# Three constants of a list scheduler: the DMA rate, the hold of the shared port and the number of passes

## The chip, the cores and the metric

The kernel runs on one core of one Trainium2 chip. The metric is the device time of one execution in microseconds (us); lower is better. Engines are named as the profile names them: PE is TensorE (PEld its weight loads), DVE VectorE, ACT ScalarE, POOL GpSimd and SP SyncE, which only issues transfers.

## The reference

All tensors are float32. Attention with a threshold feeds a dense layer with `h - tanh(h)`, and that a mixture of experts with one expert for each token.

```python
# q, k, v: (4, 8, 576, 64); tau = 0.02
scores = q @ k.transpose(0, 1, 3, 2) / 8
thresh = scores.max(-1, keepdims=True) - tau
scores = np.where(scores >= thresh, scores, -1e9)
attn = np.exp(scores - scores.max(-1, keepdims=True))
attn = attn / (attn.sum(-1, keepdims=True) + 1e-9)
x = (attn @ v).transpose(0, 2, 1, 3).reshape(2304, 512)

h = x @ w_in                         # w_in: (512, 2048)
x = (h - np.tanh(h)) @ w_out         # w_out: (2048, 512)

e_idx = np.argmax(x @ w_gate, 1)     # 8 experts; gate_w is the softmax weight of e_idx
eom = 1 / (1 + np.exp(-(x @ w_output_gate)))
out[t] = gate_w[t] * eom[t, e] * (np.maximum(x[t] @ w1[e], 0) @ w2[e])   # e = e_idx[t]
# w1: (8, 512, 1024), w2: (8, 1024, 512)
```

## The kernel before

Every operation is first recorded and only later emitted. A call of `sc.add` (class `Sched`) records an engine, a duration in ns, a due time and the buffers that are read and written. `Sched.emit` then asks `Sched.order` for one order of all of them, and each engine gets its operations in that order. On the chip an engine executes its own queue strictly in that order: an operation whose input is late holds back all that stands behind it on that engine, ready or not.

`Sched.order` builds the order by list scheduling. `Sched.greedy` plays the program through forward in time on a plan of the engines and takes, whenever an engine is free, the ready operation with the best priority. Then a pass backward in time gives new priorities, and the next forward pass uses them. After `ROUNDS` such passes (8) the order with the shortest planned span is taken. The plan knows of three costs that matter here:

- A transfer (the helper `dma`) is two entries: 500 ns on the issuing queue (1038 ns for POOL) with 480 ns of latency, and `nbytes // 360` ns on a single queue "DQ", which stands for all DMA engines, with 810 ns of latency. Each step from engine to engine adds a lag (`LAG`, 170 ns where it has no entry) and a `MARGIN` of 60 ns. Without waiting in "DQ" a transfer of 512 KB is planned to land 500 + 480 + 230 + 1456 + 810 + 230 = 3706 ns after its issue begins.
- DVE operations with two operands in SBUF, DVE casts and all POOL operations but its DMAs are marked `port`. They share one planned port; the second waits until the first is through with its whole duration.
- PE runs at half speed until it has been busy for a while.

The work itself has three stages.

- Attention, 0 to about 515 us of the profile: 32 units of one batch entry, one half of its rows and one pair of heads. Each unit computes scores on PE (`sp`, L945 for the first eight units, L936 for the others), takes the minimum of the negated scores while it copies them (DVE L954, tile `em`), the exponential on ACT (L957, tile `e`), the threshold on POOL (L965), mask and sum on DVE (L967), transposes on PE (L1000), copies to `eth` and `elh` (the helper `round_to`, ACT, L416) and the product with v (`pv`, L1047). Its inputs come through SP: `kst`, `vt`, `qh` for the first batch entry, `kr`, `vr`, `qr` for the others, which are split into a rounded part (L416) and a rest (L430 on POOL, L436 on DVE).
- The dense layer, in 9 chunks of 256 tokens (L597 `ph` and L631 `x`), part of it among the attention units and the rest until about 765 us. Its weights come in pairs of tiles `wi` and `wo`. The first visit of a pair loads four packed pieces `craw` (L532, one buffer while attention runs), unpacks each on ACT (L537) and DVE (L539, L542, L545, L548) and rounds it (L416, L430); the pair is saved to DRAM (`wsv`) and fetched again later (L519, 1 MB a tile, planned with 6000 ns more latency). The router runs beside the rest of it.
- The experts, from about 785 us: POOL gathers rows (L1453) and pairs of weight tiles `wraw` (L1304, 512 KB, two buffers), ACT (L416) or DVE (L420) rounds them and DVE (L436) makes the rest; PE computes `ph` (L1517), ACT (L1522, `hh`) and DVE (L1524, `hl`) evict it, PE computes `py` (L1545), and POOL scatters the output rows (L1557).

```python
    def dma(due, fn, r, w, nbytes, eng="SP", slack=0, after=()):
        o = sc.add(eng, 1038 if eng == "POOL" else 500, due, fn, r, w, lat=480, after=after)
        if due < 0 and not after:
            opening.append(o)
        sc.add("DQ", nbytes // 360, due, lambda: None, r, w, lat=810 + slack)
```

Of the kernel before, what the change touches and what calls it, by code (L numbers as in the profile page):

```python
# [10 lines left out]
F32 = mybir.dt.float32  # L11
F32R = mybir.dt.float32r
# [30 lines left out]
    -0.003480356204087328, 0.0012444686215600763, -0.00033910333953393964, 4.8818629992721306e-05,  # L43
)
UMAX2 = 0.0016
ROUNDS = 8
PORT = True
HALVE = 400
FULL = 8
NHH = 12  # L50
ENGINES = {
# [36 lines left out]
class Sched:  # L88
# [80 lines left out]
    def greedy(self, prio, back=False):  # L169

        ops = self.ops
        n = len(ops)
        nxt, prv = (self.pred, self.succ) if back else (self.succ, self.pred)
        left = [len(p) for p in prv]
        at = [0.0] * n
        start, end = [None] * n, [None] * n
        events = [(0.0, k) for k in range(n) if not left[k]]
        heapq.heapify(events)
        ready, free, wake = {}, {}, []
        order = []  # L180
        tick, cols, warm, port = 0, 0.0, False, 0.0
        while events or wake:
            now = events[0][0] if events and (not wake or events[0][0] <= wake[0][0]) else wake[0][0]
            touched = set()
            while events and events[0][0] <= now:
                _, k = heapq.heappop(events)
                e = ops[k].eng
                heapq.heappush(ready.setdefault(e, []), (now if e == "DQ" and not back else prio[k], k))
                touched.add(e)
            while wake and wake[0][0] <= now:  # L190
                touched.add(heapq.heappop(wake)[1])
            for e in sorted(touched):
                q = ready.get(e)
                while q and (e == "-" or free.get(e, 0.0) <= now):
                    k = heapq.heappop(q)[1]
                    dur = ops[k].dur
                    if PORT and ops[k].port:
                        begin = max(now, port)
                        port = begin + dur
                        dur = port - now  # L200
                    if e == "PE" and not back:
                        t, work = now, float(dur)
                        while work > 0:
                            b = int(t // TICK)
                            if b > tick:
                                warm = b == tick + 1 and cols >= WARM
                                tick, cols = b, 0.0
                            rate = 1.0 if warm else 0.5
                            room = (b + 1) * TICK - t
                            step = min(work, room * rate)  # L210
                            cols += step
                            work -= step
                            t = (b + 1) * TICK if work > 0 else t + step / rate
                        dur = t - now
                    start[k], end[k] = now, now + dur
                    order.append(k)
                    if e != "-":
                        free[e] = now + dur
                        heapq.heappush(wake, (now + dur, e))
                    for m, lag in nxt[k]:  # L220
                        if lag is not None:
                            t = end[k] + lag
                        elif back:
                            t = max(end[k] - ops[m].dur, now)
                        else:
                            t = now
                        if t > at[m]:
                            at[m] = t
                        left[m] -= 1
                        if not left[m]:  # L230
                            heapq.heappush(events, (max(at[m], now), m))
        assert len(order) == n, (len(order), n)
        return order, start, end
# [82 lines left out]
def tile_main(ctx, tc, qa, qb, q0, kT, vv, tau, w_in, w_out, gates, w1, w2, out, dbg=None):  # L316
    nc = tc.nc
    sc = Sched()
# [120 lines left out]
    def dma(due, fn, r, w, nbytes, eng="SP", slack=0, after=()):  # L439
        o = sc.add(eng, 1038 if eng == "POOL" else 500, due, fn, r, w, lat=480, after=after)  # L440
        if due < 0 and not after:
            opening.append(o)
        sc.add("DQ", nbytes // 360, due, lambda: None, r, w, lat=810 + slack)
        return o

    TAU = 2600
# [453 lines left out]
    def attention(ui, k0, qs):  # L900
        b, half, hp = units[ui]
        n = 320 if half else 256
        full = ui < FULL
        kb, vb_ = kst[b, hp], vts[b, hp]
        qh, ql = qs
        dt_ = F32 if full else F32R
        eth = [buf("et", f"eth{h}", 1, [P, 4, 320], dt_) for h in range(2)]
        elh = buf("et", "elh", 1, [P, 320], dt_)
        if not full:
            etl = [buf("et", f"etl{h}", 1, [P, 4, 320], F32R) for h in range(2)]  # L910
            ell = buf("et", "ell", 1, [P, 320], F32R)
        T0 = k0 * TAU
        pairs = []
        k = 0
        plist = []
        rsums = []
        for qt in range(2 + half):
# [4 lines left out]
            for h in range(1 if merged else 2):  # L922
# [5 lines left out]
                e = buf("ep", "e", 2, [P, S])  # L928
# [59 lines left out]
            for h, d in tl:  # L988
# [20 lines left out]
                for hh, cols, o, wd in outs:  # L1009
                    src = lambda pt=pt, o=o, wd=wd: pt.t[:, :, o:o + wd]  # L1010
                    hi = lambda hh=hh, cols=cols: eth[hh].t[:, :, cols]
                    if full:
                        round_to("p_h", 4 * wd, d + 400, hi, src, [pt], [(eth[hh], qt)], True)
                        continue
                    round_to("p_h", 4 * wd, d + 400, hi, src, [pt], [(eth[hh], qt)], True)
# [14 lines left out]
        round_to("p_h2", n, dl + 500, lambda: elh.t[:, 0:n], lambda: plf()[:, 0:n], [pl], [elh], True)  # L1030
        if half:
            round_to("p_h2", D, dl + 500, lambda: elh.t[D:P, 256:320], lambda: plf()[D:P, 320:384], [pl], [elh], True)
        if not full:
            rest("p_l", n, dl + 900, lambda: ell.t[:, 0:n], lambda: plf()[:, 0:n], lambda: elh.t[:, 0:n],
                 [pl, elh], [ell], True)
        if half and not full:
            rest("p_l", D, dl + 900, lambda: ell.t[D:P, 256:320], lambda: plf()[D:P, 320:384],
                 lambda: elh.t[D:P, 256:320], [pl, elh], [ell], True)
        xf = buf("ep", "xf", 1, [P, 320])
        dl += TAU  # L1040
        for h in range(2):
# [5 lines left out]
                    nc.tensor.matmul(pvf(), l_(), r_(), start=(i0 + i == 0), stop=(i0 + i == tot - 1))  # L1047

            rows = slice(h * D, (h + 1) * D)
            if full:  # L1050
                vf = lambda k: vb_.t.rearrange("p a b -> p (a b)")[:, k * P:(k + 1) * P]
                seq = [(lambda kt=kt: vf(kt), lambda kt=kt, h=h: eth[h].t[:, kt, 0:n]) for kt in range(4)]
                sc.add("PE", 2150 if half else 1730, dl, lambda seq=seq, mul=mul: mul(seq, 0, 5), [vb_, eth[h]], [pv])
# [32 lines left out]
        while o < n:  # L1086
            c, r = divmod(t0 + o, CH)
# [11 lines left out]
    starts = []  # L1099
# [27 lines left out]
    for ui, (b, half, hp) in enumerate(units):  # L1127
        sc.kind = "att"
        T0 = starts[ui] * TAU
        if ui == 0:  # L1130
            for k in range(4):
                raw_k(0, k, (starts[k] - 4) * TAU)
                raw_v(0, k, (starts[k] + 1.5) * TAU)
            qnext = raw_q(0, T0 - 4 * TAU)
        qs = qnext
        if ui + 1 < FULL:
            qnext = raw_q(ui + 1, T0 + 0.5 * TAU)
        elif ui + 1 < len(units):
            qnext = prep_q(*units[ui + 1], T0 + 0.5 * TAU)
        if ui >= FULL and half == 0:  # L1140
            prep_v(b, hp, T0 + 1.5 * TAU)
            if hp == 0:
                prep_k(b, 3, T0 + 1 * TAU)
        elif half and b + 1 < B and hp:
            prep_k(b + 1, hp - 1, T0 + 1 * TAU)
        t_done = attention(ui, starts[ui], qs)
        if ui < 4 and FULL < 8:
            prep_k(b, hp, (starts[ui + 4] - 4) * TAU)
            prep_v(b, hp, (starts[ui + 4] - 2) * TAU)
        sc.kind = "moe"  # L1150
        for c in range(NCH):
# [601 lines left out]
```

## Time and profile before

| what | value |
|---|---|
| median of the timed runs | 1059.04 us |
| those runs, lowest to highest | 1052.75 to 1061.7 us |
| the profiled execution, its own time | 1053.74 us |
| its span, first to last instruction | 1051.9 us |
| granted TensorE clock, mean | 0.997 |
| busy: PE, PEld | 1007.0 us (96%), 887.1 us (84%) |
| busy: DVE, ACT, POOL | 756.3 us (72%), 598.7 us (57%), 485.2 us (46%) |
| moved by DMA | 164.46 MB, 156 GB/s over the span |

Busy times are unions over the span, so PE was idle for 45 us of it. Matmuls overlap, so a busy PE need not be at its highest rate. The profiled execution lies 1.84 us above its span and 5.30 us below the median of the timed runs.

### The profile page before, as it was taken

How to read it: one execution, taken by the hardware profiler on the slowest of the kernel's cores; microseconds unless marked ns; L12 is line 12 of the kernel's file. 1: busy time of each engine (PE TensorE's matmuls, PEld its weight loads, DVE VectorE, ACT ScalarE, POOL GpSimd, SP SyncE). 2: the span in 40 equal slices, each digit the busy share in tenths (PEclk: the TensorE clock that was granted, in tenths of full speed). 3: DMA queues.
4: the chain of work that ended last, by engine and by line, in shares of the span. 5: the costliest groups of instructions: out<-in, count | busy, mean ns of one | idle time of the engine just before them, and what ended most of it. 6: DMA issues, size and time to landing. Idle time of an engine off the chain costs nothing.

```text
span 1051.9 us, 18625 instructions
## 1 busy us (share of the span) xinstructions
PE 1007.0 (96%) x6535; PEld 887.1 (84%) x6535; DVE 756.3 (72%) x1894; ACT 598.7 (57%) x1214; POOL 485.2 (46%) x734
## 2 busy tenths in 40 slices
PE   5899999999999999999999999999998999989997
PEld 3676888888999988999998988888986888878786
DVE  3778889987878988997757986788464666565440
ACT  2767789988988777776645544444323333243221
POOL 2347788787967777556420100110114454354311
PEclk9999999999999999999999999999999999999999
DMA  8345444446536166352194643422505655555421
GB/s 209 130 164 191 145 156 160 160 169 191 174 139 219 41 192 216 108 202 81 72 387 151 243 166 115 141 91 95 187 28 190 202 192 166 176 177 174 149 63 39
DMA packets 45624, 164.46 MB, mean 156 GB/s; under 512 B 6430, under 2 KB 6430, under 8 KB 39376
## 3 DMA queue, kind: packets, MB, share of 16 engines
q1 hardware_dynamic: 33872, 123.39, 35.3%
q0 software_dynamic: 11488, 39.53, 11.9%
q8 instruction: 53, 0.87, 0.3%
q14 instruction: 51, 0.42, 0.1%
q10 hardware_dynamic: 160, 0.26, 0.1%
HBM read 128.03 MB, written 35.85 MB: 156 GB/s over the span
## 4 chain that ended last, share of the span: by engine, by line
PE 64%; DMA 11%; issue 8%; DVE 6%; ACT 6%; POOL 3%; SPq 1%; POOLq 0%; ACTq 0%; DVEq 0%
PE ph L597 17%; PE x L631 17%; PE pv L1047 7%; DMA wraw<-in_w_dram,widx 7%; PE py L1545 5%; PE sp L936 5%; PE pt L1000 4%; PE ph L1517 2%; PE sp L945 2%; DMA craw<-in_w_in_dram 2%; DMA qr<-in_qa_dram 1%; DMA craw<-in_w_out_dram 1%; ACT eth L416 1%; ACT e L957 1%; DVE em L967 1%
## 5 line engine op out<-in xcount | busy, mean ns | idle before, releaser
L597 PE MATMUL ph<-xh,wi 128*128 128x256 f32 x1152 | 177.9, 284 | 0.0
L631 PE MATMUL x<-wo,gh 128*128 128x512 f32 x576 | 168.1, 404 | 0.0
L597 PEld LDWEIGHTS ph<-xh,wi 128*128 128x128 f32 x1152 | 155.0, 188 | 4.4
L967 DVE SCALAR_TENSOR_TENSOR em<-em,tb,e 128x576 f32<-128x576 f32 x144 | 131.2, 913 | 22.5 <-ACT e L957 15.5
L957 ACT ACTIVATE e<-em,mx 128x576 f32<-128x576 f32 x144 | 111.3, 774 | 34.4 <-DVE em L954 29.1
L954 DVE TENSOR_SCALAR_CACHE_REDUCE em<-sp 128x576 f32<-128x576 f32 x144 | 108.2, 751 | 29.3 <-PE sp L945 15.1
L418 POOL TENSOR_SCALAR gh<-u 128x512 fp32r<-128x512 f32 x53 | 39.2, 739 | 194.4 <-DVE u L620 172.4
L631 PEld LDWEIGHTS x<-wo,gh 128*128 128x128 f32 x576 | 99.8, 188 | 14.9
L1304 POOL DMA_INDIRECT wraw<-in_w_dram,widx x56 | 57.8, 1031 | 108.8 <-DVE w L436 41.7
L416 ACT ACTIVATE eth<-pt 128x512 fp32r<-128x512 f32 (+3 forms) x160 | 86.3, 552 | 18.5 <-PE pt L1000 10.3
L597 PE MATMUL ph<-xl,wi 128*128 128x256 f32 x576 | 92.7, 282 | 0.0
L631 PE MATMUL x<-wo,gl 128*128 128x512 f32 x288 | 91.7, 401 | 0.0
L610 ACT ACTIVATE u<-ph 128x512 f32<-128x512 f32 x72 | 43.0, 598 | 85.2 <-PE ph L597 83.9
L1000 PE MATMUL pt<-ident,em 128*128 128x128 f32 x576 | 86.2, 276 | 2.9 <-DVE em L967 2.8
L965 POOL TENSOR_TENSOR tb<-mx,tau_t 128x1 f32<-128x1 f32 x144 | 54.1, 376 | 68.2 <-DVE em L954 62.3
L1000 PEld LDWEIGHTS pt<-ident,em 128*128 128x128 f32 x576 | 68.8, 142 | 13.5 <-DVE em L967 3.4
L1545 PE MATMUL py<-w,hh 128*128 128x512 f32 (+3 forms) x252 | 79.2, 395 | 0.0
L618 DVE SCALAR_TENSOR_TENSOR w<-w,u 128x512 f32<-128x512 f32 x72 | 51.1, 710 | 38.3 <-ACT w L614 38.0
L597 PEld LDWEIGHTS ph<-xl,wi 128*128 128x128 f32 x576 | 78.2, 188 | 0.5
L1047 PE MATMUL pv<-eth,vt 128*128 128x256 f32 (+1 forms) x320 | 68.6, 344 | 6.3 <-ACT elh L416 5.4
L436 DVE TENSOR_TENSOR w<-wraw,w 128x512 fp32r<-128x512 f32 x98 | 64.9, 692 | 13.5 <-ACT w L416 12.2
L936 PE MATMUL sp<-kst,qh 128*128 128x288 f32 (+2 forms) x252 | 71.6, 303 | 1.8 <-DVE em L954 1.8
(368 smaller groups left out, 2393.3 us busy)
## 6 DMA issues: line engine op xcount, KB each, us to landing
wi<-wsv SPq DMA_DIRECT2D x18, 1024.0 KB, 6.4
wo<-wsv SPq DMA_DIRECT2D x18, 1024.0 KB, 5.6
craw<-in_w_in_dram SPq DMA_DIRECT2D x16, 512.0 KB, 4.3
craw<-in_w_out_dram SPq DMA_DIRECT2D x16, 512.0 KB, 3.8
kr<-in_kT_dram SPq DMA_DIRECT2D x24, 288.0 KB, 4.5
wsv<-wi SPq DMA_DIRECT2D x6, 1024.0 KB, 4.5
wsv<-wo SPq DMA_DIRECT2D x6, 1024.0 KB, 5.5
xsp<-xh SPq DMA_DIRECT2D x9, 512.0 KB, 3.0
```

The source lines that it names most:

```text
L416: return sc.add("ACT", act(n, psum), due, lambda: nc.scalar.activation(dst(), src(), AF.Copy), r, w)
L436: return sc.add(eng, dve(n, psum) + 5 if eng == "DVE" else pool_tt(n), due, lambda: e.tensor_tensor(out=dst(), in0=src(), in1=hi().bitcast ...
L597: nc.tensor.matmul(ph.t[:, j, :], wi.t[:, w_, cc * CH + j * P:cc * CH + (j + 1) * P], x_.t[:, cc, :], start=(n == 0 and cc == 0), stop=(n ...
L631: nc.tensor.matmul(x2b[c, half][t].t, g_.t[:, j, t * P:(t + 1) * P], wo.t[:, w_, j * DM:(j + 1) * DM], start=(first and n == 0 and j == 0) ...
L936: nc.tensor.matmul(sp.t[:, kb_, o:o + w], q_.t[:, q0:q0 + P], kb.t[:, hh, c0:c0 + w], start=(i == 0), stop=(i == len(todo) - 1),)
L954: sc.add("DVE", 665, d, lambda ev=ev, sp=sp, mx=mx: nc.vector.tensor_scalar(out=ev().rearrange("p (a b) -> p a b", a=2), in0=sp.t[:, :, 0: ...
L957: sc.add("ACT", 667, d + 800, lambda e=e, ev=ev, mx=mx: nc.scalar.activation(e.t, ev(), AF.Exp, bias=mx.t, scale=-1.0), [(em, h), mx], [e])
L967: sc.add("DVE", 729, d + TAU, lambda ev=ev, tb=tb, e=e, rs=rs, h=h: nc.vector.scalar_tensor_tensor(out=ev(), in0=ev(), scalar=tb.t, in1=e. ...
L1000: nc.tensor.matmul(pt.t[:, kt, :], em.t[:, c0:c0 + P], ident, is_transpose=True, start=(kt == 0), stop=(kt == 3))
L1047: nc.tensor.matmul(pvf(), l_(), r_(), start=(i0 + i == 0), stop=(i0 + i == tot - 1))
L1304: nc.gpsimd.indirect_dma_start(raw.t, None, src.rearrange("e f p n -> (e f p) n"), bass.IndirectOffsetOnAxis(ap=widx.t[:, s_:s_ + 1], axis=0),
L1545: nc.tensor.matmul(py[j].t[0:size[j]], x_(), wx(), start=(f == 0 and n == 0), stop=(f == 7 and n == 2))
```

## The change

Three constants of the plan change, and no operation, buffer or engine.

- `dma` counts a transfer at 250 bytes a ns in place of 360. 512 KB are planned to take 2097 ns on "DQ" in place of 1456, 1 MB 4194 in place of 2912.
- A POOL operation of duration `dur` holds the planned port for `dur - 160` ns (at least 30) in place of `dur`; its time on POOL stays the same. DVE operations hold it as before.
- `ROUNDS` is 24 in place of 8.

The other lines bring in a second constant `FULLV` beside `FULL`. Both are 8, so each of these conditions selects the same operations as before, in the same order of recording.

```diff
-ROUNDS = 8
+ROUNDS = 24
 PORT = True
+HOLD = 160
 HALVE = 400
-FULL = 8
+FULL, FULLV = 8,8
...
                     if PORT and ops[k].port:
                         begin = max(now, port)
-                        port = begin + dur
-                        dur = port - now
+                        port = begin + max(dur - (HOLD if e == "POOL" else 0), 30)
+                        dur += begin - now
...
-        sc.add("DQ", nbytes // 360, due, lambda: None, r, w, lat=810 + slack)
+        sc.add("DQ", nbytes // 250, due, lambda: None, r, w, lat=810 + slack)
...
-        full = ui < FULL
+        full, fullv = ui < FULL, ui < FULLV
...
                 raw_k(0, k, (starts[k] - 4) * TAU)
-                raw_v(0, k, (starts[k] + 1.5) * TAU)
+                if FULLV:
+                    raw_v(0, k, (starts[k] + 1.5) * TAU)
...
-        if ui >= FULL and half == 0:
+        if half == 0 and (b or not FULLV):
             prep_v(b, hp, T0 + 1.5 * TAU)
+        if b and half == 0:
```

## Rows read from the trace of the kernel before

**Rows 1.** Windows by stage: window, its us, busy by engine (instructions), PEclk, DMA share, GB/s

```profile
0.00:30.00 30.00, 16.59 (x53) 10.48 (x53) 13.53 (x48) 9.80 (x17) 5.63 (x23) 1.00 0.76 184
30.00:150.00 120.00, 114.30 (x616) 92.31 (x617) 95.44 (x230) 88.58 (x176) 75.50 (x132) 1.00 0.51 165
150.00:500.00 350.00, 343.47 (x2444) 318.77 (x2443) 299.01 (x707) 287.03 (x588) 259.91 (x424) 1.00 0.48 157
500.00:750.00 250.00, 249.79 (x1836) 223.08 (x1835) 188.57 (x565) 115.98 (x244) 39.54 (x55) 1.00 0.47 169
750.00:800.00 50.00, 45.39 (x295) 39.83 (x295) 25.97 (x99) 13.65 (x30) 8.67 (x9) 0.97 0.27 89
800.00:1050.00 250.00, 237.47 (x1300) 202.64 (x1298) 133.76 (x248) 83.70 (x160) 95.99 (x93) 1.00 0.48 150
```

**Rows 2.** Windows of the opening and of 535 to 550 us

```profile
0.00:25.00 25.00, 14.14 (x42) 8.64 (x42) 10.44 (x39) 7.53 (x12) 5.62 (x22) 1.00 0.91 218
20.00:30.00 10.00, 5.92 (x27) 3.81 (x25) 5.10 (x16) 3.73 (x8) 0.60 (x4) 1.00 0.48 114
...
535.00:550.00 15.00, 15.00 (x90) 13.13 (x89) 10.34 (x21) 8.61 (x18) 1.85 (x3) 1.00 1.01 401
```

**Rows 3.** Timeline of the opening: start, us, engine, line, count [idle before <-releaser]

```profile
12.40 0.66 ACT L537 ACTIVATE ct<-craw 128x512 f32<-128x512 f32 x1 [2.10 <-DMA craw<-in_w_in_dram]
...
13.89 0.75 DVE L954 TENSOR_SCALAR_CACHE_REDUCE em<-sp 128x576 f32<-128x576 f32 x1
...
14.71 2.29 PE L945 MATMUL sp<-kst,qh 128*128 128x288 f32 x4 [2.02 <-DVE em L954]
...
16.38 0.40 SPq L532 DMA_DIRECT2D craw<-in_w_in_dram  x1
...
26.19 0.66 ACT L537 ACTIVATE ct<-craw 128x512 f32<-128x512 f32 x1 [4.21 <-DMA craw<-in_w_in_dram]
26.76 0.37 ACT L416 ACTIVATE elh<-pv 128x256 f32<-128x256 f32 x1
...
27.18 1.13 PE L1047 MATMUL pv<-eth,vt 128*128 128x256 f32 x4 [2.97 <-ACT elh L416]
```

**Rows 4.** DMA issues: count, KB each, median us from issue to landing

```profile
wi<-wsv SPq DMA_DIRECT2D x18, 1024.0 KB, 6.4
...
craw<-in_w_in_dram SPq DMA_DIRECT2D x16, 512.0 KB, 4.3
...
wraw<-in_w_dram,widx POOLq DMA_INDIRECT x56, 4.4
```

**Rows 5.** Instructions of line L967: duration in ns min/median/max

```profile
L967 DVE SCALAR_TENSOR_TENSOR em<-em,tb,e x144: 792/818/1568, 10.4 to 513.0; 128x576 f32<-128x576 f32 x144
```

**Rows 6.** Timeline around 313 us, POOL and DVE

```profile
313.02 0.74 POOL L430 TENSOR_TENSOR gl<-u,gh 128x256 fp32r<-128x256 f32 x1
...
313.17 1.20 DVE L967 SCALAR_TENSOR_TENSOR em<-em,tb,e 128x576 f32<-128x576 f32 x1
```

**Rows 7.** Waits of PE from 800 us on: us in total, times, longest us

```profile
PE ph L1517 <- DVE hl L1524: 7.5, 9, 2.0
```

**Rows 8.** Timeline around 940 us, in the experts

```profile
939.40 0.63 ACT L416 ACTIVATE xl<-wraw 128x512 fp32r<-128x512 f32 x1 [4.28 <-DMA wraw<-in_w_dram,widx]
939.94 0.74 ACT L1522 ACTIVATE hh<-ph 128x320 fp32r<-128x320 f32 x2
...
941.01 0.48 DVE L1524 SCALAR_TENSOR_TENSOR hl<-ph,hh 128x320 fp32r<-128x320 f32 x1
...
941.55 0.85 PE L1517 MATMUL ph<-xh,w 128*128 128x320 f32 x4 [1.99 <-DVE hl L1524]
```

**Rows 9.** Waits at the head of SP's queue, 150 to 500 us

```profile
SPq L519 <- PE x L631: 37.3, 8, 15.5
```

**Rows 10.** Timeline around 387 us, after a late qr

```profile
386.58 0.63 ACT L416 ACTIVATE qh<-qr 128x512 fp32r<-128x512 f32 x1 [2.75 <-DMA qr<-in_qa_dram]
...
388.24 0.44 PE L1078 MATMUL pv<-ident,rb 128*128 128x128 f32 x2 [1.63 <-DVE xf L1071]
```

More of the change, by code (lines that the diff above doesn't have):

```diff
@@ L902, in attention @@
         n = 320 if half else 256
-        full = ui < FULL
+        full, fullv = ui < FULL, ui < FULLV
         kb, vb_ = kst[b, hp], vts[b, hp]
         qh, ql = qs
-        dt_ = F32 if full else F32R
+        dt_ = F32 if fullv else F32R
         eth = [buf("et", f"eth{h}", 1, [P, 4, 320], dt_) for h in range(2)]
         elh = buf("et", "elh", 1, [P, 320], dt_)
-        if not full:
+        if not fullv:
             etl = [buf("et", f"etl{h}", 1, [P, 4, 320], F32R) for h in range(2)]
@@ L1011, in attention @@
                     hi = lambda hh=hh, cols=cols: eth[hh].t[:, :, cols]
-                    if full:
+                    if fullv:
                         round_to("p_h", 4 * wd, d + 400, hi, src, [pt], [(eth[hh], qt)], True)
@@ L1032, in attention @@
             round_to("p_h2", D, dl + 500, lambda: elh.t[D:P, 256:320], lambda: plf()[D:P, 320:384], [pl], [elh], True)
-        if not full:
+        if not fullv:
             rest("p_l", n, dl + 900, lambda: ell.t[:, 0:n], lambda: plf()[:, 0:n], lambda: elh.t[:, 0:n],
                  [pl, elh], [ell], True)
-        if half and not full:
+        if half and not fullv:
             rest("p_l", D, dl + 900, lambda: ell.t[D:P, 256:320], lambda: plf()[D:P, 320:384],
@@ L1049, in attention @@
             rows = slice(h * D, (h + 1) * D)
-            if full:
+            if fullv:
                 vf = lambda k: vb_.t.rearrange("p a b -> p (a b)")[:, k * P:(k + 1) * P]
@@ L1148, in tile_main @@
             prep_k(b, hp, (starts[ui + 4] - 4) * TAU)
+        if ui < 4 and 0 < FULLV < 8:
             prep_v(b, hp, (starts[ui + 4] - 2) * TAU)
```

## The prediction

> **What bounds the kernel now.** I read the windows by stage first, because an order of work can gain only where PE waits. They show PE busy for 1007.0 of 1051.9 us, at the full granted clock in all stages but one [rows 1]. PE is idle for 13.4 us of the first 30, 5.7 us of the next 120, 6.5 us from 150 to 500, 0.2 us from 500 to 750, 4.6 us from 750 to 800 and 12.5 us from 800 to 1050. So the dense stage has nothing to give, and all that a better order can win is 38 us in the opening, the attention and the experts, less what is latency in any order.
>
> Then I read the opening by the timeline, since it has the largest loss for its length. The second `craw` load is issued at 16.38 us and ACT starts on it at 26.19 us, 9.8 us later. ACT had stood idle for 4.21 us with this unpacking step at the head of its queue; behind it stood the copy `elh`, which started at 26.76 us, and PE waited 2.97 us for that copy [rows 3]. PE's idle time from 20 to 30 us is 4.1 us [rows 2]. The same happens once before: ACT waits 2.10 us for the first `craw`, the unpacking goes ahead of the minimum on DVE at 13.89 us, and PE waits 2.02 us for that [rows 3].
>
> Last, the experts. All of PE's shown waits there are for `hl`, 7.5 us in 9 waits [rows 7]. The longest one reads like the opening: ACT stands 4.28 us before a rounding step whose gather is late, both `hh` copies stand behind it, `hl` follows at 941.01 us, PE goes on at 941.55 us after 1.99 us [rows 8]. In both stages a transfer was planned too short, its consumer came too early in an in-order queue, and ready work was held back.
>
> **The DMA rate, in the opening.** In the first 25 us the engines of the DMA are 91% busy and move 218 GB/s [rows 2], 5.45 MB in all. On the planned queue these bytes take 15.1 us at 360 bytes a ns and 21.8 us at 250, against 25 us on the chip. So the plan before has the second `craw` some 7 us too early, and the new one has it within 1 or 2 us of where it lands. ACT's two unpacking steps should then stand behind `elh` and the minimum. I take the whole 4.1 us of 20 to 30 us for the second, since DVE is busy for only 5.1 and ACT for 3.7 of these 10 us [rows 2] and nothing else is near, and 1.5 of 2.0 us for the first: 5.5 us, with bounds of 0 and 6.1 us. The weights that come later for it have room: the first four pieces are rounded by 50 us and the first dense matmul starts after 77 us. What is late next is the serial chain of scores, minimum, exponential and mask of the first unit, which no constant changes.
>
> **The DMA rate, in the experts.** A gather is planned to land 1038 + 480 + 230 + 1456 + 810 + 230 = 4244 ns after its issue begins, and 4885 ns after the change. The median of the chip is 4.4 us [rows 4], between the two, so half of the gathers land later than the plan before has them and fewer than half later than the new one does. I take 3 of the 7.5 us of PE's waits. The bounds are 7.5 us gained and 3 us lost, the latter where steps that are now planned later let the two `wraw` buffers go later and hold up the next gather on POOL.
>
> **The DMA rate, elsewhere.** Loads of 512 KB through SP are planned at 3.7 us before and 4.35 us after, and the median is 4.3 us [rows 4]: better for `craw`. From 535 to 550 us, where 1 MB tiles move, the chip reaches 401 GB/s with all DMA engines busy [rows 2]. There 250 is wrong by more than a third, but PE is idle for 0.2 us of 250 [rows 1], so I take nothing for it, with 0 and 3 us lost as bounds (twice the 1.63 us that PE waits after a late load [rows 10]).
>
> The Trainium skill (DMA: Bandwidth & Descriptors, Specifications) gives about 358 GB/s from HBM for one core and a vendor's cost model of 368 GB/s, which speaks for the old constant. By it the opening's bytes would take 15 us and the first term would be 0; the trace agrees with it only near 540 us.
>
> **The shorter hold.** A free masking step (L967) takes 818 ns by its median [rows 5]. The one that starts at 313.17 us meets a POOL rest that ends at 313.76 us, and ends itself at 314.37 us [rows 6], 0.61 us after POOL. Thus the port is given over some 0.2 us before POOL's operation is recorded as ended, and 160 ns is nearer to the chip than 0. The plan before therefore charged DVE up to 160 ns too much at each meeting, at most 144 x 0.16 = 23 us for L967 in 515 us. DVE is 80% busy from 30 to 150 us and 85% from 150 to 500 us [rows 1], so a plan that sees it 4 points freer puts DVE's steps a little earlier and PE's consumers with them. No row prices this. It can win no more than PE's idle time there, 5.7 + 6.5 = 12.2 us, most of which is single short waits; I take a quarter, 3 us. The lower bound is a loss of 6 us, four waits like the 1.63 us one [rows 10].
>
> The Trainium skill (SBUF — State Buffer, SBUF: two separate sides) says that the pair of ports is an exclusive lock held for the whole instruction. By that rule the second operation would end a full 0.82 us after POOL; the row gives 0.61 us, so here the measurement decides for the shorter hold.
>
> **24 passes.** The extra passes can only shorten the planned span, and what they are worth on the chip no row shows. They lie within the bounds above, from nothing to the rest of PE's idle time in attention.
>
> From 750 to 800 us PE waits for the router's lists and the first gathered rows, a chain with one order; I take 0, with 2 us either way.
>
> **The sum.** 5.5 + 3 + 3 = 11.5 us less. The profiled execution took 1053.74 us, of which 1051.9 us are span, so it becomes 1042.2 us. The three timed runs lie from 1052.75 to 1061.7 us; their mean with the profiled one is 1056.8 us, 3.1 us above the profiled one. A median of new runs should stand as far above, so I forecast 1045 us, with a range of its own of 1037 to 1050 us.
>
> **The rivals.**
>
> *The order hardly matters* (the change does not do on the chip what it does in the plan). Even with 250 the plan may have `craw` land at 22 to 24 us, two or three us before the chip does, and leave the unpacking ahead of `elh`; in the experts 4.9 us is still short of the late gathers, such as the one that held ACT for 4.28 us [rows 8]. Then about 2 us are won, and the time is 1056.8 - 2 = 1055 us, give or take 4. For it speaks that PE is 98% busy from 150 to 500 us and 99.9% after [rows 1]; against it, that the opening's wait is plainly one of order.
>
> *Slower: transfers put in front of others on SP.* SP issues in order too. From 150 to 500 us eight weight fetches (L519) stood at its head for `x` to be done, 37.3 us in all and 15.5 us at the longest [rows 9], and the loads of `qr`, `kr` and `vr` stand behind them. A plan that counts 1 MB at 4.2 us in place of 2.9 wants such fetches sooner. One late `qr` cost ACT 2.75 us and PE 1.63 us [rows 10]. With half of the 24 units after the first batch entry hit, that is 12 x 1.63 = 19.6 us lost; less the 8.5 us of the opening and the experts the time is 1056.8 + 11.1 = 1068 us. It decides from the seventh such unit, where 11.4 us eat the forecast's gain. Against it speaks that the plan issues a fetch only when it has the buffer free.
>
> *The port is held to the end.* If meetings like that of 313 us are the exception, each costs DVE 0.16 us that the plan now leaves out, 23 us of DVE in all. DVE has 15 to 20% of its time free in attention, so I let a quarter through to PE: 1056.8 + 6 = 1063 us. This is the rule of the Trainium skill's page SBUF — State Buffer cited above. Against it speaks the one meeting shown, where the masking step ends 0.61 us after POOL [rows 6].
>
> **How the numbers follow.** Chances: the forecast 0.52, hardly any effect 0.33, late loads 0.11, the full hold 0.04. About 1% is what a measurement of this kernel can tell from no change; from 1059.04 us the limits are 1048.4 and 1069.6 us. Four fifths of the forecast's chance and a tenth of the second case lie below the first: 0.45 faster. The late loads can hit anything from 7 to 24 units, 1057 to 1088 us, and two thirds of their chance lie above the second limit or near it, with half of the fourth case: 0.09 slower. The rest, 0.46, is within 1%. The range of 1034 to 1060 us takes in the forecast with a further 3 us from its bounds below and the second case above, and leaves out the third and fourth cases (0.15) and the largest gains (0.05).
>
> **What would show it.** In the new profile ACT's wait for `craw` before 30 us should be under 1 us and PE's busy time in the first 30 us should rise from 16.6 to about 21. In the experts PE's waits for `hl` should fall from 7.5 to about 4.5 us. The steps L967 keep their median of 0.82 us, and PE's idle time from 30 to 500 us falls from 12.2 to about 9. From 500 to 750 us PE stays without gaps. The prediction is wrong if the opening's stall only moves to another load, or if SP's waits at L519 grow and PE waits for steps behind `qr` or `kr`.

## The result, and the profile after

| | median of the runs | lowest to highest | runs | profiled execution | its span |
|---|---|---|---|---|---|
| before, in the same comparison | 1055.89 us | 1050.65 to 1061.7 | 4 | 1053.74 us | 1051.9 us |
| after | 1043.15 us | 1042.46 to 1044.73 | 4 | 1044.73 us | 1042.6 us |

The ratio is 0.9893, with an interval of 0.9857 to 0.9929: a little over 1% faster. 1045 us were forecast. The total came out by an accident, though: several errors cancelled, and the rest of this document is about them. The lines of the kernel after are one higher than those of before as far as the dense layer, and four higher in the experts.

The windows by stage of the kernel after answer to [rows 1]:

```profile
0.00:30.00 30.00, 21.08 (x88) 15.12 (x89) 17.16 (x58) 14.70 (x27) 7.43 (x26) 1.00 0.74 189
30.00:150.00 120.00, 116.74 (x656) 96.30 (x655) 103.32 (x237) 93.32 (x189) 84.81 (x140) 1.00 0.53 169
150.00:500.00 350.00, 343.26 (x2428) 316.56 (x2426) 311.79 (x712) 284.44 (x580) 258.31 (x419) 1.00 0.49 159
500.00:750.00 250.00, 244.57 (x1783) 216.75 (x1781) 183.97 (x546) 110.60 (x234) 34.38 (x48) 0.99 0.46 164
750.00:800.00 50.00, 46.58 (x308) 40.98 (x308) 25.40 (x98) 13.71 (x31) 8.68 (x9) 1.00 0.26 89
800.00:1042.00 242.00, 232.68 (x1284) 202.05 (x1282) 133.61 (x248) 83.73 (x160) 98.94 (x93) 0.99 0.50 155
```

PE's idle time falls from 13.4 to 8.9 us in the opening, from 12.2 to 10.0 us between 30 and 500 us, and from 12.5 to 9.3 us at the end (of these, 4.9 and 5.7 us lie behind the last `py`). But from 500 to 750 us, where it was 0.2 us, it is now 5.4 us. A window holds slightly different work in the two kernels, so the times at which the same instruction starts say better where the lead is won and lost:

| start of (us) | before | after | lead |
|---|---|---|---|
| the 9th mask (L967, after L968) | 39.31 | 33.76 | 5.6 |
| the last, 144th mask | 513.00 | 504.07 | 8.9 |
| the first `py` of the experts (L1545, after L1549) | 783.97 | 783.40 | 0.6 |
| end of the last `py` | 1045.13 | 1036.29 | 8.8 |
| end of the span | 1051.9 | 1042.6 | 9.3 |

Attention wins 8.9 us, the dense stage loses 8.4 of them, and the experts win 8.3 again. How the 8.9 us divide between the opening and the rest of attention is looser: from the 5th to the 15th mask the lead is anywhere from 5.6 to 7.8 us, and near the 50th it is 17.7 us, as the masks shift among the dense layer's work.

**The opening.** The timeline of the kernel after, with the steps that answer to [rows 3]:

```profile
11.19 0.67 ACT L538 ACTIVATE ct<-craw 128x512 f32<-128x512 f32 x1 [1.07 <-DMA craw<-in_w_in_dram]
...
14.72 1.24 PE L946 MATMUL sp<-kst,qh 128*128 128x288 f32 x4 [0.90 <-DVE em L955]
...
16.56 0.52 SPq L533 DMA_DIRECT2D craw<-in_w_in_dram  x1
...
19.64 0.38 ACT L417 ACTIVATE elh<-pv 128x256 f32<-128x256 f32 x1 [0.67 <-PE pv L1028]
...
25.35 0.66 ACT L538 ACTIVATE ct<-craw 128x512 f32<-128x512 f32 x1
```

The second load starts as late as before (16.56 against 16.38 us), and its unpacking starts only 0.8 us sooner (25.35 against 26.19 us). But `elh` now stands ahead of the unpacking and runs at 19.64 us in place of 26.76 us, and PE doesn't wait for it. PE's wait near 14.7 us is 0.90 in place of 2.02 us. The windows that answer to the first two of [rows 2] show that the transfers themselves did not change, 220 GB/s against 218, while PE's 20 to 30 us are full:

```profile
0.00:25.00 25.00, 16.11 (x64) 11.17 (x65) 13.36 (x49) 10.65 (x19) 6.72 (x25) 1.00 0.87 220
20.00:30.00 10.00, 9.97 (x51) 8.22 (x51) 6.89 (x18) 6.80 (x15) 1.35 (x5) 1.00 0.44 114
```

**The dense stage.** First PE's waits from 500 us on (us in total, times, longest), which answer to [rows 7]; then the timeline of the kernel after around the loss:

```profile
PE ph L1521 <- issue: 3.6, 2, 2.6
PE ph L598 <- DVE u L621: 2.6, 1, 2.6
...
PE ph L598 <- ACT wi L417: 1.4, 1, 1.4
PE x L632 <- ACT wo L417: 1.1, 1, 1.1
```

```profile
539.45 5.74 SPq L533 DMA_DIRECT2D craw<-in_w_out_dram  x2
...
564.95 0.66 ACT L538 ACTIVATE ct<-craw 128x512 f32<-128x512 f32 x1
567.12 0.66 ACT L538 ACTIVATE ct<-craw 128x512 f32<-128x512 f32 x1
569.36 3.06 SPq L533 DMA_DIRECT2D craw<-in_w_in_dram  x2
...
573.41 1.31 PE L632 MATMUL x<-wo,gh 128*128 128x512 f32 x3 [1.10 <-ACT wo L417]
...
577.61 3.07 SPq L533 DMA_DIRECT2D craw<-in_w_out_dram  x2
...
580.99 0.50 PE L598 MATMUL ph<-xh,wi 128*128 128x256 f32 x2 [1.38 <-ACT wi L417]
...
589.23 1.00 PE L598 MATMUL ph<-xh,wi 128*128 128x256 f32 x4 [2.56 <-DVE u L621]
```

Two `craw` pieces are issued by the first of these lines, at 539.45 and 544.86 us. Among the 1 MB tiles these two take longer than the 3.9 us that such loads take by their median in this profile. Their times from issue to landing (L533, issued from 535 to 550 us):

```profile
DMA to landing us min/median/max: 6.6/8.7/10.8
```

So they land at 550.2 and 551.5 us, and ACT unpacks them only at 565 and 567 us: they lie in their buffers for some 15 us. `craw` has two buffers in this stage, and the loads of the last pair wait on SP for them; SP's waits there, and PE's window, are

```profile
SPq L533 <- DVE ct L549: 33.7, 5, 19.0
```

```profile
560.00:600.00 40.00, 34.90 (x205) 30.34 (x203) 32.61 (x57) 19.76 (x39) 1.29 (x2) 0.96 0.47 163
586.00:594.00 8.00, 5.44 (x30) 5.10 (x29) 7.97 (x15) 4.73 (x11) 0.65 (x1) 0.79 0.50 203
```

The wait on SP is the loss: SP stands up to 19.0 us until DVE has finished with a buffer. Then the weights `wo` and `wi` come late one after the other, and so does `u` from DVE, which is now full (7.97 of 8 us). PE is idle for 5.1 us, and behind its wait of 2.56 us the granted clock falls to 0.79 in the mean of 8 us, which is 3.4 us at 1.2 GHz and costs about half of that. 5.1 + 1.7 = 6.8 of the 8.4 us are in these rows; the other 1.6 us are not placed here.

**The experts.** No wait for `hl` is left among PE's waits; 7.5 us stood in [rows 7]. Against that stand two new waits before `ph`, 3.6 us in all, which the list above puts down to `issue`, that is, to nothing that the profile shows.

**Late `qr`, and the mask.** Two waits from attention, SP's from 150 to 500 us, which answers to [rows 9], and ACT's from 120 to 500 us, and the duration of the mask, which answers to [rows 5]:

```profile
SPq L520 <- PE x L632: 46.1, 8, 11.8
```

```profile
ACT qh L417 <- DMA qr<-in_qa_dram: 1.3, 1, 1.3
```

```profile
L968 DVE SCALAR_TENSOR_TENSOR em<-em,tb,e x144: 789/825/1492, 10.2 to 504.1; 128x576 f32<-128x576 f32 x144
```

SP's fetches stand somewhat longer in all, but only one `qr` is late, where ACT waited 5.8 us for three before. The median of the mask is that of before, but its mean is not. The pages' rows, before and after (us busy, mean ns of one, idle time before them):

```profile
L967 DVE SCALAR_TENSOR_TENSOR em<-em,tb,e 128x576 f32<-128x576 f32 x144 | 131.2, 913 | 22.5 <-ACT e L957 15.5
L968 DVE SCALAR_TENSOR_TENSOR em<-em,tb,e 128x576 f32<-128x576 f32 x144 | 143.3, 997 | 30.0 <-ACT e L958 16.0
```

The masks take 12.1 us more in all, since more of them meet POOL: 39 took over 0.9 us before, 63 after.

### The profile page after: what moved, and what is told of

Its sections match the earlier page's. It is cut to its first block, busy times and chain, and to the rows that moved or that the text cites. A ratio compares the mean times of both kernels' runs of the same rounds, so it can differ in the third digit from the quotient of the medians.

```text
span 1042.6 us, 18602 instructions
## 1 busy us (share of the span) xinstructions
PE 1004.9 (96%) x6535; PEld 887.8 (85%) x6535; DVE 775.3 (74%) x1894; ACT 600.5 (58%) x1214; POOL 492.5 (47%) x734
## 3 DMA queue, kind: packets, MB, share of 16 engines
q0 software_dynamic: 11488, 39.53, 12.2%
## 4 chain that ended last, share of the span: by engine, by line
PE 72%; DVE 9%; issue 6%; ACT 5%; DMA 4%; POOL 2%; POOLq 0%; ACTq 0%; SPq 0%; DVEq 0%
PE ph L598 16%; PE x L632 16%; PE py L1549 9%; PE pv L1048 7%; PE ph L1521 7%; PE sp L937 4%; PE pt L1001 4%; PE sp L946 3%; DVE em L968 3%; DMA wraw<-in_w_dram,widx 2%; DVE em L955 2%; ACT e L958 1%; PE ph L1234 1%; ACT eth L417 1%; PE x L692 1%
## 5 line engine op out<-in xcount | busy, mean ns | idle before, releaser
L598 PE MATMUL ph<-xh,wi 128*128 128x256 f32 x1152 | 182.1, 286 | 4.0 <-DVE u L621 2.6
L598 PEld LDWEIGHTS ph<-xh,wi 128*128 128x128 f32 x1152 | 157.1, 189 | 10.0 <-DVE u L621 3.2
L968 DVE SCALAR_TENSOR_TENSOR em<-em,tb,e 128x576 f32<-128x576 f32 x144 | 143.3, 997 | 30.0 <-ACT e L958 16.0
L1549 PE MATMUL py<-w,hh 128*128 128x512 f32 (+3 forms) x252 | 79.4, 396 | 0.0
```

What stands on the lines that cost most here:

```text
L598: nc.tensor.matmul(ph.t[:, j, :], wi.t[:, w_, cc * CH + j * P:cc * CH + (j + 1) * P], x_.t[:, cc, :], start=(n == 0 and cc == 0), stop=(n ...
L968: sc.add("DVE", 729, d + TAU, lambda ev=ev, tb=tb, e=e, rs=rs, h=h: nc.vector.scalar_tensor_tensor(out=ev(), in0=ev(), scalar=tb.t, in1=e. ...
L1549: nc.tensor.matmul(py[j].t[0:size[j]], x_(), wx(), start=(f == 0 and n == 0), stop=(f == 7 and n == 2))
```

## The experiments

The theory was that the rate of 250 makes the gain by letting the plan see late loads where they are late (the opening, the experts), and that the same rate loses in the dense stage, where 1 MB tiles move faster. The rivals: the shorter hold or the passes make it, or any new order would have come out somewhere within such a spread. The kernel before has the ratio 1 in each comparison; its medians there were 1054.07 us (22 runs), 1053.84 us (10) and 1052.9 us (20).

### One constant at a time

Against the kernel after; `HOLD = 0` and 360 are the costs of before:

```diff
f_rate, f_rate_hold, f_hold:   -ROUNDS = 24
                               +ROUNDS = 8
f_rate:                        -HOLD = 160
                               +HOLD = 0
f_hold, f_hold24:              -        sc.add("DQ", nbytes // 250, ...)
                               +        sc.add("DQ", nbytes // 360, ...)
```

**f_rate**, the rate alone:

> Only the DMA rate is changed (250 bytes a ns; old hold, 8 passes). Theory A (each constant is worth what it removes of late inputs): the stall on the second craw is gone, PE is busy for about 21 us of the first 30, its waits for hl in the experts fall below 4 us, and the time is about 8 us under the kernel before. Theory B (any new order is a draw from a spread of some 10 us, whatever the constant): the opening may go either way and the time is anywhere from 15 us under to 8 us over.

**f_hold**, the hold alone:

> Only the hold of the port is changed (160 ns; 360 bytes a ns, 8 passes). Theory A: the craw stall stays (ACT waits for 3 us or more for craw before 30 us, PE busy under 18 us of the first 30), the waits for hl in the experts stay above 5 us, attention gains up to 3 us, and the time is 0 to 4 us under the kernel before. Theory B: no relation, 15 us under to 8 us over.

**f_rate_hold**, both, with 8 passes:

> Rate and hold as in the changed kernel, but 8 passes. Theory A: opening and experts as in the changed kernel, time within 3 us of it (about 12 us under the kernel before). Theory B: time differs from the changed kernel by 5 us or more, either way.

**f_hold24**, the hold and 24 passes, without the rate:

> Hold of 160 ns at the old rate, 24 passes, which select another order than 8 do. If the shorter hold itself harms at the old rate (it starts DVE's steps and loads sooner and meets the late transfers more often): 1060 us or more again, with over 9 us of waits for transfers between 120 and 400 us. If the slower run with 8 passes was one draw of an order: within 6 us of the kernel before, on either side.

Measured:

| kernel | rate, hold, passes | median us | ratio, interval |
|---|---|---|---|
| f_rate | 250, 0, 8 | 1044.36 | 0.9910, 0.9879 to 0.9942 |
| f_rate_hold | 250, 160, 8 | 1043.53 | 0.9906, 0.9875 to 0.9937 |
| after | 250, 160, 24 | 1043.15 | 0.9893, 0.9857 to 0.9929 |
| f_hold | 360, 160, 8 | 1064.19 | 1.0110, 1.0053 to 1.0168 |
| f_hold24 | 360, 160, 24 | 1052.20 | 0.9984, 0.9970 to 0.9997 |

The rate alone gives the gain, within what the medians can tell. It also makes most of the loss in the dense stage, 5.8 us from the last mask to the first `py` (507.04 and 783.80 us); the windows of f_rate there are, with PE 5 us idle as in the kernel after but without the fall of the clock:

```profile
560.00:600.00 40.00, 35.05 (x221) 30.61 (x220) 32.94 (x58) 19.16 (x36) 1.90 (x3) 1.00 0.44 157
586.00:594.00 8.00, 5.62 (x49) 5.42 (x48) 7.30 (x13) 6.28 (x13) 0.66 (x1) 1.00 0.82 329
```

Without the rate, the hold keeps both of the old stalls. ACT's wait in the first 30 us and PE's in the experts, of f_hold:

```profile
ACT ct L538 <- DMA craw<-in_w_in_dram: 6.9, 2, 4.6
```

```profile
PE ph L1521 <- DVE hl L1528: 4.2, 5, 1.6
```

and of f_hold24:

```profile
PE ph L1521 <- DVE hl L1528: 7.3, 8, 1.6
```

f_hold was a miss of both readings, 10 us over the kernel before. f_hold and f_hold24 differ by 12 us for a constant that says nothing of the machine. The loss of f_hold lies in attention: its span from the 9th to the last mask is 484.6 us, against 473.7 before and 474.4 in f_hold24, and ACT stands there 12.2 us for transfers (`craw` 6.2, `kr` 4.5, `qr` 1.5), against 6.9 us in f_hold24. So it is the order that these 8 passes happen to settle on, not the price of a hold. With the costs of before, 24 passes select the same order of all engines as 8, so there is no kernel with the passes alone.

### Where each lead is made and lost

The three `g_` kernels record the same work, plan it twice, and emit the first part by one plan and the next by the other. `at_b` is the barrier between attention and the rest of the dense layer, `at_f` the one ahead of the experts.

```diff
-        sc.emit(ROUNDS)
+        sc.emit_parts((("new", at_b), ("old", at_f), ("new", None)))   # g_new_old_new
+        sc.emit_parts((("new", at_b), ("old", None)))                  # g_new_old_old
+        sc.emit_parts((("old", at_f), ("new", None)))                  # g_old_old_new
...
+    def emit_parts(self, parts):
+        plans = {"old": self.plan(360, 0, 8), "new": self.plan(250, 160, 24)}
+        done = set()
+        for which, stop in parts:
+            for o in plans[which]:
+                if o not in done:
...
+                if o is stop:
+                    break
```

**g_new_old_old**, the new order in attention alone:

> The order of the changed kernel while attention runs, that of the kernel before for the rest. Theory A: the lead of about 9 us at the end of attention is kept to the end: 1045 us. Rival: it is lost behind attention, 1052 us or more.

**g_old_old_new**, the new order in the experts alone:

> The order of the kernel before up to the experts, that of the changed kernel in them. Theory A: the waits of PE for hl fall from 7.5 us to under 2 us and the experts take some 8 us less: 1046 us. Rival (the experts profit only because they begin in another state of the transfers): under 3 us gained, 1051 us or more.

**g_new_old_new**, the new order except in the dense stage:

> The order of the changed kernel while attention runs, that of the kernel before from there to the experts, and that of the changed kernel in the experts. Theory A (each stage keeps its own gain; the new rate loses 8 us at 565 to 614 us in the changed kernel, because the unpacking of the last two weight pairs is planned too late): no idle time of PE between 560 and 600 us, and 1035 us, 8 us under the changed kernel. Rival (a lead from attention is bound to vanish there, since the weights' transfers set the time): PE idles there again and the time is within 2 us of the changed kernel.

| kernel | median us | ratio, interval | last mask | first `py` | end of span |
|---|---|---|---|---|---|
| g_new_old_old | 1046.84 | 0.9927, 0.9901 to 0.9953 | 504.17 | 775.18 | 1047.3 |
| g_old_old_new | 1041.51 | 0.9871, 0.9830 to 0.9912 | 519.80 | 790.75 | 1046.8 |
| g_new_old_new | 1033.03 | 0.9799, 0.9761 to 0.9836 | 504.95 | 775.95 | 1030.7 |

By the medians, attention is worth 1053.84 - 1046.84 = 7.0 us and the experts 12.3 us; together that is 19.3, and the two together measured 20.8 us. The kernel after has 12.7 us of these in its own comparison, so its dense stage costs 8 us. (For the experts alone 8 us were expected, and 12.3 came.) The last two columns of times say the same within one execution: with the old order in the dense stage the lead of attention arrives whole at the first `py` (775.95 us, 8.0 before the 783.97 us of before). What the old order does there shows in the timeline, the window and SP's wait of g_new_old_new (27 lines higher than after):

```profile
552.37 1.21 ACT L565 ACTIVATE ct<-craw 128x512 f32<-128x512 f32 x2
...
556.62 3.20 SPq L560 DMA_DIRECT2D craw<-in_w_in_dram  x2
...
564.81 4.35 SPq L560 DMA_DIRECT2D craw<-in_w_out_dram  x2
```

```profile
560.00:600.00 40.00, 40.00 (x278) 35.77 (x277) 36.64 (x66) 22.07 (x44) 5.06 (x5) 1.00 0.62 217
```

```profile
SPq L560 <- DVE ct L576: 17.9, 5, 6.1
```

Its own two pieces, from issue to landing (L560, issued at 539.70 and 541.03 us):

```profile
DMA to landing us min/median/max: 10.7/10.8/10.8
```

They land at 550.5 and 551.8 us, no sooner than in the kernel after, but they are unpacked 12.6 us sooner, the last loads start 12.7 and 12.8 us sooner, and PE has no gap. g_old_old_new is by its profile the worst of its four runs (1048.6 us; the others are from 1037.95 us), so its last columns are not set against those of the others (the profile of g_new_old_old, 1049.38 us, is the worst of seven); but its list of waits shows none for `hl`, and its experts take 1046.8 - 790.75 = 256.1 us from the first `py` to the end, 11.9 less than the 267.9 us of before.

### The rate by size

**sized** gives transfers of 1 MB and more 400 bytes a ns, near what they move at, and leaves the others at 250:

```diff
-        sc.add("DQ", nbytes // 250, ...)
+        sc.add("DQ", nbytes // (400 if nbytes >= 1 << 20 else 250), ...)
```

> As the changed kernel, but transfers of 1 MB are planned at 400 bytes a ns, as fast as they move at 535 to 550 us, and all others at 250. Theory A: the unpacking at 565 us comes sooner, PE does not idle from 560 to 600 us, opening and experts stay as in the changed kernel: 1036 us, 7 us under it. Rival (orders are draws): within 5 us of the changed kernel either way, with PE's idle time elsewhere.

**sized_hold0** is the same with `HOLD = 0`:

> The rates by size (400 bytes a ns for 1 MB, 250 for the rest) with the old hold. If the hold has a worth of its own, as I predicted, 2 to 4 us slower than with 160 ns: 1035 to 1037 us. If it has none once the rate is right: within 2 us of 1033 us.

**rate300** has one rate for all, between the two:

```diff
-        sc.add("DQ", nbytes // 250, ...)
+        sc.add("DQ", nbytes // 300, ...)
```

> As the changed kernel, but 300 bytes a ns for all transfers. Theory A (the rate is worth what it removes of late inputs): the second craw is planned some 3 us too early, so ACT waits 1 to 3 us for it before 30 us; the unpacking at 565 us comes sooner, so less than half of the idle time of PE from 560 to 600 us is left; 1039 us. Rival (draws): 1045 us or more.

| kernel | median us | lowest to highest | ratio, interval |
|---|---|---|---|
| sized | 1033.13 | 1031.28 to 1033.68 | 0.9797, 0.9760 to 0.9834 |
| sized_hold0 | 1035.29 | 1033.41 to 1035.70 | 0.9831, 0.9815 to 0.9848 |
| rate300 | 1046.88 | 1042.77 to 1049.65 | 0.9945, 0.9916 to 0.9975 |

sized beats both kernels, by 10 us that after. Its window of the loss and PE's wait in the experts:

```profile
560.00:600.00 40.00, 40.00 (x277) 35.70 (x276) 37.25 (x71) 22.85 (x45) 3.35 (x4) 1.00 0.63 219
```

```profile
PE ph L1521 <- DVE hl L1528: 1.6, 2, 1.1
```

PE is full from 560 to 600 us, and little is left of `hl`. Only the planned duration of the 1 MB transfers differs from the kernel after, so it is their 4.2 us in place of 2.6 that put the unpacking late. sized_hold0 is 2.2 us above sized by the medians, at the lower end of what was expected of a hold with a worth of its own, and the two intervals overlap.

rate300 was a miss. 1039 us were expected and 1046.88 came: a rate between the two doesn't give half of both gains. The loss of the dense stage is nearly gone, as expected (PE is idle for 0.4 us from 560 to 600 us), but most of the stalls of the opening and the experts is back: the 9th mask, at 37.32 us, leads by 2.0 us in place of 5.6, and these are ACT's wait for `craw` in the first 30 us and PE's for `hl`:

```profile
ACT ct L538 <- DMA craw<-in_w_in_dram: 5.1, 2, 2.8
```

```profile
PE ph L1521 <- DVE hl L1528: 5.6, 7, 1.5
```

### The opening by hand

**s_late** is the kernel before, with its own plan, but two of the unpacking steps are emitted later by fixed times, and **s_late4** moves all four of the first pair:

```diff
-        sc.emit(ROUNDS)
+        sc.emit_late({('piece', 0, 1): 900, ('piece', 0, 2): 4200})               # s_late
+        sc.emit_late({('piece', 0, 1): 900, ('piece', 0, 2): 4200,
+                      ('piece', 0, 3): 6500, ('piece', 0, 4): 6500})              # s_late4
```

> The kernel before with its own order, except that the unpacking of the first craw piece is moved 0.9 us later in the order and that of the second 4.2 us later (what depends on them moves along). Theory A: ACT's wait for the second craw before 30 us is gone, PE is busy for about 20 us of the first 30, the eighth masking step starts 4 to 5 us sooner than before, and the time is 4 to 5 us under the kernel before. Rival: the lead is used up later, as the changed kernel's was between 565 and 614 us, and the time is within 2 us of the kernel before.

> As the earlier run that moved two craw pieces, but all four pieces of the first pair are moved: 0.9, 4.2, 6.5 and 6.5 us later in the order of the kernel before. There the third piece stalled ACT and DVE at 36.5 us, PE stood for 6.0 us and its clock fell. Theory A (the lead is kept once no piece heads a queue before it has landed): no wait of PE over 2 us between 20 and 60 us, no fall of the clock there, the eighth masking step 4 us sooner than before, and 1049 to 1050 us, 4 to 5 under the kernel before. Rival (the weights now come too late for the dense steps and the lead is lost): within 2 us of the kernel before.

| kernel | median us | ratio, interval | 9th mask |
|---|---|---|---|
| s_late | 1057.42 | 1.0030, 0.9997 to 1.0062 | 41.18 |
| s_late4 | 1054.75 | 1.0023, 1.0007 to 1.0039 | 35.10 |

Neither gained. (The expectations count this mask as the eighth.) The timeline of s_late shows why (its lines are 17 to 20 higher than those of before):

```profile
22.04 0.38 ACT L433 ACTIVATE elh<-pv 128x256 f32<-128x256 f32 x1 [0.67 <-PE pv L1047]
...
36.53 0.66 ACT L556 ACTIVATE ct<-craw 128x512 f32<-128x512 f32 x1 [2.35 <-DMA craw<-in_w_out_dram]
37.23 0.43 DVE L558 TENSOR_SCALAR ct<-ct 128x512 f32<-128x512 f32 x1 [4.99 <-ACT ct L556]
...
39.72 1.09 PE L1020 MATMUL pt<-ident,em 128*128 128x128 f32 x4 [5.98 <-DVE em L987]
```

`elh` runs 4.7 us sooner, as the prediction has it, but the third piece is now the one that is planned too early: DVE stands 4.99 us before its step, the mask stands behind that step, and PE waits 5.98 us. In s_late4 that one is gone too, the 9th mask starts 4.2 us earlier than before, and PE then waits 1.57, 3.01, 1.57 and 1.52 us between 48 and 79 us. So the stall is one of order, and moving it by hand shows that; but the lead is gone by the 15th mask. That it would be kept only by a plan that is right about all the loads behind it is argued, not shown.

## Why the prediction was right, and where it was not

**The DMA rate, in the opening: right.** 5.5 us were forecast and the 9th mask is 5.6 us early (its neighbours up to 7.8). ACT's wait for `craw` before 30 us is 1.1 us (under 1 forecast) and PE's busy time 21.1 us (21 forecast). Of its two parts the larger one came whole (PE is idle for 0.03 us from 20 to 30 us), the smaller one 1.1 of 1.5 us. The weights that are now unpacked later hold nothing up: the first dense matmul starts at 66.3 us in place of 77.8. The graft g_new_old_new and f_rate, whose 9th masks are 4.6 and 4.2 us early, show that it is the rate and the order, not the transfers.

**The shorter hold: right in sum by luck.** From the 9th to the last mask the kernel after wins a further 3.4 us, near the 3 us forecast, and PE's idle time from 30 to 500 us is 10.0 us where 9 were forecast. But the other kernels do not repeat it. By the last mask f_rate, without the hold, leads the kernel before by 6.0 us and f_rate_hold, with it, by 4.7; with the rates by size the lead is 5.4 us without it (sized_hold0) and 10.0 with it (sized); at the old rate the two orders with the hold are 11.9 and 1.3 us behind. In the total the hold is worth about 2 us at the right rate (sized against sized_hold0), which these runs don't tell from the scatter of orders. The meeting of [rows 6], on which the term rests, is the rule in the traces: 35 of the 39 masks over 0.9 us of the kernel before, and 54 of the 63 after, started while a POOL operation ran and end 0.60 to 0.62 us behind it. What the term left out is that a plan that counts less for a meeting has more of them: the mean of the mask is 913 to 943 ns in the kernels without the hold (before, f_rate, sized_hold0) and 960 to 997 ns in the six with it. So the rival of the full hold, which would have needed longer masks or a slower kernel, got longer masks; but each meeting ends as the prediction read it, and the kernel was not slower.

**The DMA rate, in the experts: mis-sized.** 3 of 7.5 us were forecast; all 7.5 us of waits for `hl` went, and the stage is 8.3 us shorter from the first to the last `py`. PE's idle time between them is 7.0 us in place of 12.3, and 3.0 us of the gain are in shorter busy time, which no row here explains. In the grafts, to the end of the span, the same order wins 13.2 and 11.9 us (254.8 and 256.1 against 267.9), so the 8.7 us of the kernel after are the low end of it. The prediction judged by the median how many gathers land after their planned time, and called it half before and fewer than half after; in the kernel before 45 of the 56 took longer than 4.24 us, and only 13 longer than 4.89 us. So what decides, as far as these numbers tell, is how far into the tail the plan reaches: ACT stood for `wraw` 89.7 us in 44 waits before and 52.3 us in 30 after. The dose shows in PE's waits for `hl`: from 4.2 to 9.8 us in the kernels whose experts are planned at 360, 5.6 at 300, and 0 to 1.6 at 250.

**The DMA rate, elsewhere: the step that failed.** "PE is idle for 0.2 us of 250, so I take nothing for it, with 0 and 3 us lost as bounds": the loss was 8.4 us, and PE did not stay without gaps. A full PE says that a stage has nothing to give; it says nothing of what it has to lose. The prediction saw that 250 is wrong there by a third, and priced it by one late load in attention. What it missed is the second way in which a planned time does harm: a load that is planned too late is consumed too late, its buffer is held, and the next load waits for that on SP. Shown by g_new_old_new and by sized, which take only the order or only the duration back and reach 1033 us both. That the planned queue backs up and so moves the unpacking is argued from sized and from the landings, which are alike in the graft and in the kernel after; the plan itself is no view of the trace.

**24 passes: right for the total.** f_rate_hold and after are 0.4 us apart. Their orders differ, though: by the last mask the one leads by 4.7 us and the other by 8.9.

**The rivals.** *The order hardly matters* fell, at 1055 us. *Transfers in front of others on SP* fell: the waits at L520 grew from 37.3 to 46.1 us, but one `qr` was late, and PE waited at most 0.5 us behind it. (The prediction's 1057 us for seven units take off the forecast's whole gain, its 1068 us for twelve only 8.5 us; with 8.5 in both the first is 1060 us. Nothing here hangs on it.) What came nearest to it was another place, the ring of `craw`. A rival that was not named is true in part: single orders scatter, by 12 us between f_hold and f_hold24, so the total of one order says little of a constant; what stands is what a trace localises and a graft repeats.

**The sum.** By the prediction's steps it was 5.5 + 3 + 3 = 11.5 us, and the profiled execution should have taken 1042.2 us; it took 1044.73. Measured between the two profiles: 5.6 + 3.4 - 8.4 + 8.3 and 0.4 behind the last `py`, 9.3 us. The 3.1 us that were added for the median did not come, as the median of after lies 1.6 us below its profiled execution. (The 38 us that it took for the most that could be won held 4.9 us behind the last `py`, in which PE has nothing left to do.) So three misses cancelled: 5 us too little for the experts, 8 us of loss that had no price, and 5 us between a profiled execution and a median.

## What to carry to other kernels

In a list-scheduled kernel a planned transfer that is too short stalls an in-order queue, and one that is too long holds a buffer and delays the next load; so give the plan the time that each size of transfer shows in its own stage, not one rate. Ask of a stage without idle time what it can lose, and follow the lead of an early stage by the start of the same instruction to the end. Judge a constant of the plan by several orders or by grafting one stage, since the next order alone can be 10 us away for no reason that these runs show. A median that stays can hide a cost: look at the mean too, as for the masks here.

## What the runs showed of the hardware

The same DMA engines move very different rates: 220 GB/s in the first 25 us, 87% busy, and in the windows of the kernel after where 1 MB tiles move, the second of which answers to the last of [rows 2],

```profile
530.00:545.00 15.00, 15.00 (x90) 13.14 (x89) 11.53 (x20) 8.06 (x18) 0.62 (x1) 1.00 1.02 415
535.00:550.00 15.00, 15.00 (x96) 13.42 (x95) 11.69 (x23) 5.76 (x12) 1.35 (x2) 1.00 0.99 385
```

The Trainium skill (DMA: Bandwidth & Descriptors, Specifications) gives about 358 GB/s as the HBM limit of one core, half of what a stack has for two; both rows are above it, and the plan of sized rests on the rows.

A stall of PE can cost twice, for the clock may fall behind it. In s_late, behind the wait of 5.98 us, the stretch from 30 to 150 us shows it in the column PEclk:

```profile
30.00:150.00 120.00, 109.79 (x577) 88.50 (x576) 91.84 (x219) 84.50 (x167) 71.39 (x125) 0.96 0.48 156
```

0.96 in the mean of 120 us is some 10 us at 1.2 GHz in place of 2.4. In the kernel after, the wait of 2.56 us at 589 us was followed by such a fall, in f_rate a loss of the same 5 us in the same place was not; what decides between them no run here shows. And the orders differ in how steady they are: the runs of before spread over 9 to 14 us in the three larger comparisons, the four of after over 2.3 us and the four of sized over 2.4, but the four of g_old_old_new over 10.7, for a reason that stays open.
